# LN1 on GpSimd, paired tail rows, a spectrum by n mod 4 and loads in pieces, in a one-core H3 block

## The chip, the cores and the metric

The kernel runs on one core of one Trainium2 chip. The metric is the device time of one execution in microseconds (us); of several runs the median counts. The profile is that of one execution, and its times are counted from its first instruction.

## The reference

The kernel computes a layer of two parts for 2048 positions of width 640, in bf16: a long convolution with gating (H3), and a feed-forward part (SwiGLU).

```python
x  = A_q
q  = layernorm(x)                                  # LN1: (x - mean) / sqrt(var + 1e-5)
ks = sum(pad(k)[t:t+S] * shift_k[:, 3-t] for t in range(4))
kv = ks * v
y  = irfft(rfft(pad(kv, 2*S)) * rfft(pad(ssm_k, 2*S)))[:S] + kv * ssm_D
h  = x + q * y
z  = layernorm(h)                                  # LN2
out = h + (silu(z @ w_gate) * (z @ w_up)) @ w_down # 640 -> 1728 -> 640
```

## The kernel before, in words

**Blocks.** The 2048 positions are cut into four blocks of 512, each held as 128 partitions by 4 rows r (position 4p + r). In the program's names x, k, v and g are a block of A_q, A_k, A_v and A_ssm_k; kv is the product of the reference. The long convolution is made of spectra of single blocks: for block j the spectrum X(j) of kv and the spectrum G(j) of g are computed by matrix products with a constant WF (line L347), G is combined into windows H, and the products X(i)H(j-i) are summed into a buffer A on VectorE (`mac`, L588, L609, L612). `inverse` turns A back with a constant WI (L679 to L715 on VectorE, L727 on TensorE), multiplies by LN1's result (L741) and adds to x, which gives h. `turn_h` applies LN2 and transposes (L765, or by DMA, L758). `ffn` makes 27 products of 5 matmuls of 512 columns per block (gate and up, `whole`, L831), silu and product (L820 to L848), and the down projection (L888) with 14 pieces of 128 rows of w_down per output row; the last piece has 64 rows of data and 64 rows of zeros, in `tail` and in `wd`, which GpSimd fills (L951, L952).

**Spectra.** `transform` has two ways. `halves_of` uses that the sum over the 4 rows splits into even and odd rows: 32 matmuls of 320 columns for a spectrum, then one VectorE operation over 2560 elements. "four" uses n mod 4: 16 matmuls, then two subtractions over 1280 elements and two operations over 2560 elements. `SUM` names the spectra that go by "four": X3 and the inverses of blocks 2 and 3. Each group of matmuls ends in PSUM and is copied out by ScalarE (L339) or VectorE (L340).

**The short convolution** is done on TensorE (L567): for each row 40 matmuls with 64 contraction rows, in two halves of the partitions, against diagonal matrices `diag` made of the taps (L947). One such run of 40 is called a convolution group here, four per block.

**Layer norms.** ScalarE sums (L656) and sums of squares (L625), then `norm` makes the inverse root by nine small VectorE steps (L642 to L650, four values a partition), and `applied` scales a row on ScalarE (L667) or VectorE (L664).

**What sets the order.** The program first lists all operations with what they read and write, and then emits them in the order of a table of numbers, `ORDER`; a minus sign stands for an operation's other engine (for example ScalarE's copy on VectorE). Every engine works through its own instructions in that order, and waits where a buffer or a value isn't there. There are four PSUM buffers (`ps`), 13 large SBUF buffers (`big`), 8 of spectra (`S`) and 5 rows (`row`). Loads and DMA transposes are issued by SyncE (SP), sums by DMA (L255), some weight loads (L789) and the additions to the output (L895) by GpSimd (POOL), each queue in order.

The lines that make the two kinds of products and the tail:

```python
# L347, spectrum:      matmul(ps[:, h, 0:320], WF[:, r, c, :], src[:, r, h*320:(h+1)*320])
# L831, gate and up:   matmul(ps[:, i, :], w[:, k, off:off+128], hT[:, k, :])        # 512 columns
# L888, down:          matmul(ps[:, hf, to:to+n], tT or tail, wd[:, c, ...])         # 320 columns
```

## Time and profile before

| | before |
|---|---|
| median of 3 runs | 258.8 us (258.7 to 258.85) |
| the profiled execution's own time | 257.87 us |
| its span, first to last instruction | 256.2 us |
| TensorE (PE) busy | 247.3 us |
| VectorE (DVE) busy | 194.1 us |
| ScalarE (ACT) busy | 168.8 us |
| GpSimd (POOL) busy | 49.6 us |
| granted TensorE clock | 1.000 |

PE is the matmul side of TensorE, PEld its weight loads, which overlap with matmuls. A row of the timeline gives start, duration, engine, line, operation, output and input, how often, and in brackets the idle time before it with what ended it. The chain of waits is followed back from the last instruction; its pieces have start, duration and name. Busy times of PE count pipelined matmuls as long as they are in flight, so work is better counted by the distance of starts. "The first gate and up product" is the first L831 of block 0; it divides the program into a start, in which TensorE waits often, and the rest.

### The profile page before, as it was taken

The numbers are of one execution on the slowest core, as the hardware profiler recorded it, in microseconds if no ns is written. First come the engines' busy times: TensorE is split into PE (matmuls) and PEld (weight loads), VectorE is DVE, ScalarE is ACT, GpSimd is POOL, SyncE is SP. The second block draws the span as 40 slices with busy tenths as digits, with TensorE's granted clock in tenths as the row PEclk, the third lists the DMA queues.
The fourth block names the chain that finished last, engine by engine and source line by source line (L and its number), as shares of the span: only waits on it lengthen the run. The fifth ranks groups of instructions, "written<-read, shape, count | busy, mean of one in ns | idle before, by whom it ended". The sixth has DMA issues, their size and how long they took to land.

```text
span 256.2 us, 5180 instructions
## 1 busy us (share of the span) xinstructions
PE 247.3 (97%) x2086; PEld 149.1 (58%) x2102; DVE 194.1 (76%) x302; ACT 168.8 (66%) x289; POOL 49.6 (19%) x67
## 2 busy tenths in 40 slices
PE   6999999899999999999999999999999999999994
PEld 5676776744556477644554577544457754444672
DVE  0799999999998999998998999999989200004223
ACT  2899999895979997667579675343765344446100
POOL 6900100530300010021321610316003023000000
PEclk9999999999999999999999999999999999999999
DMA  6986998897999768699899684889915318000002
GB/s 204 397 305 142 301 144 187 254 249 179 240 269 316 171 172 153 105 208 225 220 171 175 91 199 95 144 177 252 225 32 132 75 31 102 0 0 3 0 26 77
DMA packets 51250, 41.29 MB, mean 161 GB/s; under 512 B 25429, under 2 KB 45210, under 8 KB 51226
## 3 DMA queue, kind: packets, MB, share of 16 engines
q1 hardware_dynamic: 44304, 26.53, 38.6%
q0 software_dynamic: 6912, 14.42, 30.5%
q8 instruction: 16, 0.26, 0.4%
q14 instruction: 8, 0.07, 0.1%
q10 hardware_dynamic: 10, 0.01, 0.0%
HBM read 21.94 MB, written 4.59 MB: 104 GB/s over the span
## 4 chain that ended last, share of the span: by engine, by line
PE 90%; ACT 3%; DMA 2%; DVE 2%; issue 1%; DVEq 0%; POOLq 0%
PE ps L831 45%; PE ps L888 24%; PE ps L347 10%; PE ps L727 5%; PE ps L567 4%; ACT S L339 3%; DMA row<-in_A_ssm_D_dram 2%; PE ps L426 1%; DVE tT L825 0%; DVE big L767 0%; PE ps L765 0%; DVE S L340 0%; PE ps L530 0%; DVE big L432 0%; DVE row L905 0%
## 5 line engine op out<-in xcount | busy, mean ns | idle before, releaser
L831 PE MATMUL ps<-big,big 128*128 128x512 bf16 x524 | 118.5, 379 | 0.9 <-issue 0.2
L831 PEld LDWEIGHTS <-big 128*128 128x128 bf16 x540 | 52.4, 98 | 60.4
L888 PE MATMUL ps<-wd,tT 128*128 128x320 bf16 (+2 forms) x416 | 60.2, 299 | 0.2 <-DVE tT L825 0.2
L888 PEld LDWEIGHTS <-tT 128*128 128x128 bf16 x416 | 40.6, 98 | 16.8 <-DVE tT L825 0.6
L825 DVE TENSOR_TENSOR tT<-tT,co 128x2048 bf16<-128x2048 bf16 x12 | 14.6, 1220 | 32.2 <-ACT co L820 32.1
L347 PE MATMUL ps<-big,WF 128*128 128x320 bf16 x240 | 38.3, 299 | 0.3 <-ACT co L820 0.3
L822 ACT ACTIVATE tT<-ps 128x1024 bf16<-128x1024 f32 x24 | 24.6, 1027 | 17.7 <-PE ps L831 17.6
L609 DVE TENSOR_TENSOR big<-S,S 128x2560 bf16<-128x2560 bf16 x24 | 35.0, 1483 | 1.0 <-DMA S<-big 1.0
L339 ACT ACTIVATE S<-ps 128x640 bf16<-128x640 f32 (+1 forms) x57 | 31.6, 619 | 4.1 <-PE ps L347 4.0
L820 ACT CAST co<-ps 128x1024 bf16<-128x1024 f32 x24 | 24.2, 1013 | 13.7 <-PE ps L831 12.8
L347 PEld LDWEIGHTS <-WF 128*128 128x128 bf16 x240 | 22.9, 97 | 11.3 <-issue 1.6
L255 POOL DMA_DIRECT2D S<-big x9 | 10.9, 1208 | 82.7 <-DVE sm L644 28.3
L625 ACT ACTIVATE row<-big 128x640 bf16<-128x640 bf16 x32 | 23.4, 734 | 2.8 <-DMA big<-row 2.7
L612 DVE TENSOR_TENSOR S<-S,big 128x2560 bf16<-128x2560 bf16 x16 | 23.7, 1486 | 0.2
L667 ACT ACTIVATE row<-big,sm 128x640 bf16<-128x640 bf16 x22 | 19.5, 918 | 3.1 <-DVE sm L650 3.1
L895 POOL DMA_DIRECT2D out_dram<-row x12 | 12.8, 1356 | 15.8 <-ACT row L894 15.8
L741 DVE SCALAR_TENSOR_TENSOR row<-row,ps 128x640 bf16<-128x640 bf16 x16 | 12.9, 818 | 2.9 <-PE ps L727 2.3
L894 ACT CAST row<-ps 128x640 bf16<-128x640 f32 x12 | 8.0, 692 | 10.8 <-PE ps L888 9.0
L255 POOL DMA_DIRECT2D S<-S x5 | 6.6, 1328 | 41.5 <-ACT S L339 33.2
L567 PEld LDWEIGHTS <-T 64*128 64x128 bf16 x640 | 11.3, 110 | 3.5 <-issue 3.0
L567 PE MATMUL ps<-diag,T 64*128 64x64 bf16 x640 | 12.6, 194 | 0.0
L588 DVE TENSOR_TENSOR big<-S,S 128x2560 bf16<-128x2560 bf16 (+1 forms) x10 | 12.2, 1218 | 0.0
(87 smaller groups left out, 247.2 us busy)
## 6 DMA issues: line engine op xcount, KB each, us to landing
S<-big POOLq DMA_DIRECT2D x9, 640.0 KB, 6.6
big<-in_B_w_up_dram SPq DMA_DIRECT2D x10, 320.0 KB, 5.0
big<-in_B_w_gate_dram SPq DMA_DIRECT2D x10, 320.0 KB, 5.3
S<-S POOLq DMA_DIRECT2D x5, 640.0 KB, 9.1
big<-in_A_ssm_k_dram SPq DMA_DIRECT2D x4, 640.0 KB, 9.3
big<-in_A_q_dram SPq DMA_DIRECT2D x4, 640.0 KB, 6.7
big<-in_A_v_dram SPq DMA_DIRECT2D x4, 640.0 KB, 8.6
wd<-in_B_w_down_dram SPq DMA_DIRECT2D x1, 2080.0 KB, 15.2
```

Of the source, the lines that this page charges most:

```text
L255: nc.gpsimd.dma_start(out=to(), in_=what(), accum_op=ALU.add, max_dma_last_dim=2 * D * 2)
L339: plan.add("act", 700 if n else 430, lambda: nc.scalar.activation(dst(), src(), ACT.Copy, scale=by), [ps], [part], (), ("dve", 820 if n el ...
L347: nc.tensor.matmul(ap(ps)[:, h, 0:NH], ap(WF)[:, r, c, :], ap(src)[:, r, h * NH:(h + 1) * NH], start=(first and i == 0), stop=(last and i ...
L567: nc.tensor.matmul(out()[:, b, c, :], k, ap(diag)[at, c, t, :], start=(t == 0), stop=(t == 3))
L609: dve(1490, lambda b=b, xs=xs, hs=hs: nc.vector.tensor_mul(flat2(b), X.part(xs), H.part(hs)), [X.at(xs), H.at(hs)], [b], [A.b])
L612: f(A.part(dst), A.part(dst), flat2(b))
L625: act(825, lambda r=r, junk=junk: nc.scalar.activation(ap(junk), ap(x)[:, r, :], ACT.Square, scale=D ** -0.5, accum_out=sm(s, 1)[:, r:r + ...
L667: nc.scalar.activation(ap(row), ap(x)[:, r, :], ACT.Identity, bias=sm(s, 5)[:, r:r + 1], scale=sm(s, 4)[:, r:r + 1])
L820: act(1010, lambda ps=ps: nc.scalar.copy(ap(co)[:, at:at + 2, :], ap(ps)), src, [(co, gi % 2)])
L822: act(1010, lambda ps=ps: nc.scalar.activation(ap(tT)[:, c:c + 2, :], ap(ps), ACT.Silu), src, [done(range(c, c + 2), ROWS)])
L831: nc.tensor.matmul(ap(ps)[:, i, :], ap(w)[:, k, off:off + P], ap(hT)[:, k, :], start=(k == 0), stop=(k == KT - 1))
L888: nc.tensor.matmul(ap(ps)[:, hf, to:to + n], t, ap(wd)[:, c, col + (hf - hs[0]) * NH:col + (hf - hs[0]) * NH + n], start=(c == order[0]), ...
```

## The change

- LN1 of blocks 1 to 3 goes by `apart`, five GpSimd operations, one of them a power with exponent -0.5 from a new constant `root`, in place of nine VectorE steps. Block 0's LN1 and every LN2 stay.
- The down projection has 13 whole pieces. The 64 rows of the last piece are loaded twice into `wd`, to partitions 0 to 63 and 64 to 127; `tail` is half as long, with the second half of the positions in the upper partitions, and four matmuls with 64 contraction rows serve two output rows (`halves`, L900 of the new program). Odd blocks go through the pieces backwards. The fills with zeros go.
- The spectrum of block 2's kv goes by "four".
- A_k and A_v of block 0 are loaded in two parts, A_ssm_k of block 0 in parts of two and three column groups, and WF in two.
- The last output row is still cut into 384 and 256 columns, now with the 256 last.
- `ORDER` is a new table. In it block 0's keys come before its filter, 16 of the 20 operations that make `diag` go from GpSimd to VectorE, and the convolution groups of block 2 stand among block 0's gate and up products; before, they stood ahead of the first of them.

```diff
-SUM = {'X3': 'four', 'i2': 'four', 'i3': 'four', 'G3': 'four'}
+SUM = {'X3': 'four', 'i2': 'four', 'i3': 'four', 'G3': 'four', 'X2': 'four'}
-LASTCUT = 2
+LASTCUT = 384
+GPIECES = ((0, 2), (2, KT))
 ORDER = [
-    21, 0, 20, 2, 1, 14, 4, 5, 6, 7, 19, 3, 47, 45, 51, 46, 48, 49, 53, 17, -51, 8, 27, 52, 29, 28, -31, 25, 201, 23, -27,
+    0, 4, 15, 16, 1, 2, 5, 6, 9, 3, 7, 24, 28, 12, 17, 32, 22, -14, 29, 30, -34, 31, 23, 14, 26, 54, 11, -28, 34, 19, 57,
...
+    root = fixed([P, R], FP32, "root")
-    tail = fixed([P, BLK], BF16, "tail")
+    tail = fixed([P, BLK // 2], BF16, "tail")
...
-    def load_t(src, j):
+    def load_t(src, j, n=1):
         b = new("ld")
-        load(MB, 5120, lambda: nc.sync.dma_start(out=rd(b), in_=block(src, j)), [b])
+        for lo in range(0, R, R // n):
+            load(MB // n, 5120 // n, lambda lo=lo: nc.sync.dma_start(out=rd(b)[:, lo:lo + R // n, :], in_=block(src, j)[:, lo:lo + R // n, :]),
+                 [(b, frozenset(range(lo, lo + R // n)))])
         return b
...
+    def apart(s):
+        v = nc.gpsimd
+        def go():
+            v.tensor_mul(sm(s, 6), sm(s, 2), sm(s, 2))
+            v.tensor_sub(sm(s, 3), sm(s, 1), sm(s, 6))
+            v.tensor_scalar(sm(s, 3), sm(s, 3), EPS, None, op0=ALU.add)
+            v.tensor_tensor(sm(s, 4), sm(s, 3), ap(root), op=ALU.pow)
+            v.tensor_mul(sm(s, 5), sm(s, 2), sm(s, 4))
+        plan.add("pool", 5500, go, [root], [s])
...
-        norm(s)
+        if plan.block:
+            apart(s)
+        else:
+            norm(s)
         return s
...
-            act(600, lambda ps=ps: nc.scalar.activation(ap(tail)[0:64, :], ap(ps)[0:64, 0, :], ACT.Silu), [(ps, 0)], [done_tail(ROWS)], [tT])
-            act(590, lambda ps=ps: nc.scalar.copy(ap(co)[0:64, 1, :], ap(ps)[64:P, 0, :]), [(ps, 0)], [(co, 1)])
-            dve(420, lambda: nc.vector.tensor_mul(ap(tail)[0:64, :], ap(tail)[0:64, :], ap(co)[0:64, 1, :]), [(co, 1)], [done_tail(ROWS)], [tT])
+            for i in range(2):
+                at, cols = slice(i * H2, (i + 1) * H2), slice(i * half_of, (i + 1) * half_of)
+                act(395, lambda ps=ps, at=at, cols=cols: nc.scalar.activation(ap(tail)[at, :], ap(ps)[0:H2, 0, cols], ACT.Silu), [(ps, 0)], [(tail, i)], [tT])
+                act(390, lambda ps=ps, at=at, cols=cols: nc.scalar.copy(ap(co)[at, 1, 0:half_of], ap(ps)[H2:P, 0, cols]), [(ps, 0)], [(co, 1 + i)])
+            dve(290, lambda: nc.vector.tensor_mul(ap(tail), ap(tail), ap(co)[:, 1, 0:half_of]), [(co, 1), (co, 2)], [tail], [tT])
...
+        order = list(range(NC_FULL))[::1 if j % 2 == 0 else -1]
+        for pair in ((ROWS[0], ROWS[2]), (ROWS[1], ROWS[3])):
...
+            def both(rows=rows):
+                i = ROWS.index(rows[0][0])
+                for k in range(2):
+                    for b, (r, ps, cuts, last) in enumerate(rows):
+                        ps, hf, n, col = cuts[k]
+                        at = slice(b * H2, (b + 1) * H2)
+                        nc.tensor.matmul(ap(ps)[:, hf, 0:n], ap(tail)[at, i * P:(i + 1) * P], ap(wd)[at, NC_FULL, col:col + n],
+                                         start=j % 2 == 1, stop=j % 2 == 0, skip_group_check=True)
...
-    plan.add("pool", 600, lambda: nc.gpsimd.memset(ap(tail)[64:P, :], 0.0), [ident], [(tail, "zero")])
-    plan.add("pool", 600, lambda: nc.gpsimd.memset(ap(wd)[64:P, NC_FULL, :], 0.0), [ident], [(wd, "zero")])
```

The first place is TensorE at the end of block 0's down projection (`tT_85` holds 13 pieces of the product of silu and up, `tail` the last; `ps_93` to `ps_96` are the four PSUM buffers). Before:

```order
L888 MATMUL ps_96<-wd,tT_85 128x320
L888 LDWEIGHTS tail
L888 MATMUL ps_96<-wd,tail 128x320
L888 LDWEIGHTS tail
L888 MATMUL ps_96<-wd,tail 128x320
L888 LDWEIGHTS tT_85
L888 MATMUL ps_95<-wd,tT_85 128x320
```

And in the changed program:

```order
L915 MATMUL ps_94<-wd,tT_85 128x320
L900 LDWEIGHTS tail
L900 MATMUL ps_95<-wd,tail 128x320
L900 LDWEIGHTS tail
L900 MATMUL ps_93<-wd,tail 128x320
L900 LDWEIGHTS tail
L900 MATMUL ps_95<-wd,tail 128x320
L900 LDWEIGHTS tail
L900 MATMUL ps_93<-wd,tail 128x320
L915 LDWEIGHTS tT_85
```

Two tail matmuls for one output row become four, with 64 contraction rows each, for two output rows; there are 8 such groups in the program.

The second place is ScalarE in the start, in the changed program: `S_65` takes block 0's X, `S_64` block 0's G, `big_72` is the transposed filter of block 1. Before, the 16 copies into `S_64` were all made, by both engines, ahead of the first into `S_65`.

```order
L344 ACTIVATE S_65<-ps_96 128x320
L344 ACTIVATE S_65<-ps_95 128x320
L344 ACTIVATE S_64<-ps_93 128x320
L344 ACTIVATE S_64<-ps_94 128x320
L344 ACTIVATE S_64<-ps_96 128x320
L435 COPY big_72<-ps_95 128x640
L344 ACTIVATE S_64<-ps_96 128x320
```

G's second half of the columns is now copied behind X's first half.

The third place is GpSimd's queue at LN1 of block 2 (`sm_102`), in the changed program; before, the queue had none of the five L660 to L664.

```order
L925 DMA out_dram<-row_88 128x640
L660 TENSOR_TENSOR sm_102<-sm_102 128x4
L661 TENSOR_TENSOR sm_102<-sm_102 128x4
L662 TENSOR_SCALAR sm_102<-sm_102 128x4
L663 TENSOR_TENSOR sm_102<-sm_102,root 128x4
L664 TENSOR_TENSOR sm_102<-sm_102 128x4
L925 DMA out_dram<-row_90 128x640
L925 DMA out_dram<-row_89 128x640
L256 DMA big_73<-row_90 128x640
```

They stand between the additions of block 0's output rows; behind them come two more of these additions and the sums by DMA into h of block 2.

145 lines of the change are left out of this document (75 added, 70 removed), and 78 rows, old and new, of the table ORDER.

## The prediction

> **What bounds the kernel now.** I read the page's shares and its slices first, then busy times by stage, then the chain of waits, and at last the timeline where TensorE waits.
>
> ```profile
> PE 247.3 (97%) x2086; PEld 149.1 (58%) x2102; DVE 194.1 (76%) x302; ACT 168.8 (66%) x289; POOL 49.6 (19%) x67
> DVE  0799999999998999998998999999989200004223
> ACT  2899999895979997667579675343765344446100
> ```
>
> ```profile
> core 0: us, PE busy (x) PEld busy (x) DVE busy (x) ACT busy (x) POOL busy (x), PEclk, DMA share, GB/s
> 6.00:18.00 12.00, 11.48 (x252) 8.98 (x252) 9.91 (x23) 10.55 (x28) 6.68 (x16) 1.00 1.01 384
> 18.00:34.00 16.00, 15.48 (x264) 11.34 (x256) 15.96 (x30) 15.83 (x35) 1.28 (x1) 1.00 0.82 205
> 34.00:51.00 17.00, 16.35 (x271) 12.28 (x267) 16.28 (x39) 15.75 (x30) 3.36 (x4) 1.00 0.93 193
> 51.00:89.00 38.00, 37.79 (x198) 19.63 (x201) 36.83 (x48) 33.86 (x62) 4.82 (x5) 1.00 0.98 240
> 150.00:208.00 58.00, 57.84 (x347) 33.94 (x348) 48.30 (x73) 29.74 (x42) 10.79 (x11) 1.00 0.66 139
> ```
>
> TensorE is the bound of the whole, but not of every stage. From 18 to 51 us ScalarE is busy 31.58 of 33 us and VectorE 32.24. The reader is to see that this start isn't set by matmuls alone. From 51 us on TensorE hardly stops. So I split the time at the first gate and up product. The chain of waits gives that point and the prices of the work behind it:
>
> ```profile
> 50.83 0.32 PE ps L831
> ...
> 123.43 0.79 PE ps L567 x40
> 124.23 0.32 PE ps L831
> 124.55 0.05 issue
> 124.60 2.97 PE ps L831 x13
> 127.57 0.80 PE ps L567 x40
> ...
> 161.97 10.74 PE ps L831 x49
> 172.71 0.05 issue
> 172.76 10.74 PE ps L831 x49
> ...
> 193.02 15.26 PE ps L888 x112
> ...
> 252.67 0.56 DVE row L905
> ```
>
> A 512-column matmul costs (172.76 - 161.97)/50 = 0.2158 us (the "issue" stands for a matmul without a record), one of 320 columns 15.26/112 = 0.1363. From one convolution group to the next 4.14 us pass, with 15 gate and up matmuls between by the program (14 recorded, one under "issue"), 3.24 us; so a group of 40 among such matmuls costs 0.90. Its weight loads are spaced closer:
>
> ```profile
> 123.36 0.75 PEld L567 LDWEIGHTS <-T 64*128 64x128 bf16 x40 [0.42 <-issue]
> ```
>
> With 0.11 us for the last, (0.75 - 0.11)/39 is 0.0164 a matmul, 0.65 for 40. The other 0.25 is what going to 64 contraction rows and back costs; the 0.42 idle shows that the loads can't run ahead there.
>
> Count of the work behind 50.83, with the numbers of matmuls from the program: 540 gate and up 116.5, 448 down 61.0, 80 spectrum and 64 inverse 19.6, 4 convolution groups 3.6; together 200.7. To 252.67 are 201.8 us. So 1.1 us idle is all that can be won there without taking work away. Half of it stands in one place:
>
> ```profile
> 144.78 1.04 PE L347 MATMUL ps<-big,WF 128*128 128x320 bf16 x6 [0.29 <-ACT co L820]
> 146.05 2.89 PE L888 MATMUL ps<-wd,tT 128*128 128x320 bf16 x20 [0.23 <-DVE tT L825]
> ```
>
> **The change part by part.**
>
> **Block 2's spectrum:** 16 matmuls fewer, 16 x 0.1363 = 2.18 us of TensorE. Behind the split, though, the new order has 16 matmuls of other spectra that stood ahead of it before: 80 spectrum matmuls before and after. So the saving is taken in the start, where other engines set the end. VectorE gets two subtractions more, off TensorE's path.
>
> **Paired tails:** 32 tail matmuls, 32 x 0.1363 = 4.36 us, become 8 groups. In a group two pairs run side by side, 2 x 0.1363 = 0.27, if halves overlap as in the convolution, where 64 columns pass every 0.0164 us and one half alone needs a fifth of a 320-column matmul, 0.027. The way into 64 rows and back adds 0.25. I take 0.52 a group, 4.2 in all: a saving of 0.2. Bounds: without the way in and out 2.2 saved; with no overlap, 4 x 0.1363 + 0.25 = 0.80 a group, 2.0 lost. The Trainium skill, page "TensorEngine Tiling (Array Packing)", promises up to 2x for at most 64 contraction rows in "Theoretical Speedup"; by that alone the sum would be 2.0 better. The same page says in "Key Properties" that a change of the tiling mode drains the engine, which speaks against so short groups; the 0.25 of this trace agrees with the drain.
>
> **Moved convolution:** 8 groups instead of 4 stand behind the split, two of them directly behind another in each half of the count. 8 x 0.65 + 6 x 0.25 = 6.7 against 3.6: 3.1 more there. I take it in full; at worst each pays its own way in and out, 0.5 more.
>
> **The start:** what sets the split is ScalarE, which copies nearly all of the spectra out of PSUM. Its steps, from start to start:
>
> ```profile
> 6.71 1.88 ACT L430 COPY big<-ps 128x640 bf16<-128x640 bf16 x3 [3.82 <-PE ps L426]
> 16.55 0.72 ACT L625 ACTIVATE row<-big 128x640 bf16<-128x640 bf16 x1
> 17.27 0.72 ACT L625 ACTIVATE row<-big 128x640 bf16<-128x640 bf16 x1
> 17.98 2.74 ACT L339 ACTIVATE S<-ps 128x320 bf16<-128x320 f32 x7
> ```
>
> ```profile
> 43.49 2.46 ACT L339 ACTIVATE S<-ps 128x640 bf16<-128x640 f32 x4
> 45.32 1.15 DVE L664 TENSOR_SCALAR row<-big,sm 128x640 bf16<-128x640 bf16 x3
> 45.83 1.30 ACT L576 CAST big<-ps 128x640 bf16<-128x640 f32 x2
> 46.99 1.12 POOL L952 MEMSET wd<- 64x640 bf16 x1
> 47.07 1.54 DVE L664 TENSOR_SCALAR row<-big,sm 128x640 bf16<-128x640 bf16 x1
> 49.53 0.69 ACT L767 COPY big<-ps 128x640 bf16<-128x640 bf16 x1 [1.11 <-PE ps L765]
> ```
>
> A copy of 320 columns takes 0.39, of 640 columns 0.60, a convolution's copy 0.64. Up to the last copy of block 0's transposed h, ScalarE gets 6 copies of 320 more (+2.3), 5 of 640 fewer (-3.0), 3 convolution copies fewer (-1.9), and two copies of transposes more (+1.2): -1.4. The fourth L664 took 1.54 us where the others took 0.4, while GpSimd filled `wd`; the fill goes, and with it the 1.11 that ScalarE waits before the last copy. Its sums for LN1 of block 0 move into the time in which it waits for the filter. The first bytes come in smaller pieces:
>
> ```profile
> 5.92 1.15 PEld L426 LDWEIGHTS <-big 128*128 128x128 bf16 x20 [1.39 <-DMA big<-in_A_ssm_k_dram]
> 7.67 0.70 PEld L530 LDWEIGHTS <-big 128*128 128x128 bf16 x11 [0.60 <-DMA big<-in_A_k_dram]
> ```
>
> The first 640 KB were there at 5.9, the next at 7.7. Half of the keys may be there a us earlier, but the sums need x, which is second and comes at 7.7; by then ScalarE has done 1.4 us of copies, as much as before by 8.1. I take no gain from the pieces. The split moves by -1.4 - 1.1 = -2.5, to 48.3. Bounds: 1.4 us earlier still, if the early copies count in full (46.9); 50.5, if the eight G copies behind X's first half (8 x 0.39 = 3.1 before X is whole) find no work of TensorE ready, and 2.2 of the 2.5 are lost.
>
> **LN1 on GpSimd:** 27 VectorE steps go, 0.2 each as these two stand apart, 5.4 us of an engine that TensorE rarely waits for. Fifteen GpSimd operations come:
>
> ```profile
> 44.26 0.16 DVE L645 TENSOR_TENSOR sm<-sm 128x4 f32<-128x4 f32 x1
> 44.45 0.16 DVE L646 SCALAR_TENSOR_TENSOR sm<-sm 128x4 f32<-128x4 f32 x1
> ```
>
> ```profile
> L942 POOL TENSOR_TENSOR row<-ident 128x64 bf16<-128x64 bf16 x1 | 0.3, 307 | 0.1
> ```
>
> A power isn't in the trace. Five at 0.31 are 1.5; the fill's 1.12 each would be 5.6. The nearer row is the tensor operation of 64 columns. In the new order some ten ScalarE instructions of 0.6 to 1.0 us stand between the last sum and the first use of block 2's, so 5.6 is hidden, and I cost it at nothing; without that cover it is 1.5 for each of three blocks. Queued behind it are two additions to the output and the sums into h, which ScalarE's row buffers wait for.
>
> **Idle and end:** the VectorE chain to the last inverse gets shorter, so I take 0.6 instead of 1.1 idle behind the split (-0.5), with 0 and 3 as bounds. The last addition has 256 instead of 384 columns: from the 0.56 above to about two thirds of it, -0.1 to -0.2; its output DMA is shorter too. I take -0.2.
>
> **Sum:** split -2.5, convolution +3.1, tails -0.2, idle -0.5, end -0.2: -0.3 us. The profiled execution, 257.87 (span 256.2), would take 257.6; it ran 0.9 under the median of 258.8. On the median that is 258.5. A measurement of this kernel can tell about 0.2%, 0.5 us, from no change.
>
> **The rivals.** First, a faster tail and start: the 64-row groups pay no way in and out between 320-column matmuls (-2.0 more), or the early keys count in full (-1.4 more). For it: the start's DMA is what the first copies wait for, 3.82 us. Against it: 0.25 at each group in the trace. With either alone 257.1 or 256.5, with both 255.1. (The first half of this is what the 2x of the Trainium skill's page "TensorEngine Tiling (Array Packing)", section "Theoretical Speedup", would give.)
>
> Second, slower: ScalarE's queue in the start. G's second half is copied behind X's first, so X is whole only when 24 copies of 320 are through instead of 16, and VectorE's products and the inverse wait for it. If the split comes later than 48.6, the moved convolution, which is then paid behind it, is more than what was gained. At 50.5 the sum is +1.9: 260.7. For it: VectorE is full there too; against it: ScalarE has less to do in all.
>
> Third, slower: a sum by DMA or the GpSimd norms hold up VectorE's products of block 1, and TensorE waits for the inverse; 1 to 2 us, 259.5 to 260.5. For it: the DMA share is 0.98 from 51 to 89 us; against it: VectorE has fewer steps.
>
> Fourth, the moved convolution does what such a move would be for: it fills waits of TensorE behind the split. Against it: there are only 1.1 us of them.
>
> **How the numbers follow.** The forecast, an even trade, 0.42, with its own range 257.6 to 259.4; the first rival with the fourth 0.36; the second 0.14, the third 0.08. The forecast's 0.42 falls to faster 0.13, same 0.20 and slower 0.09; the first gives faster 0.34 and same 0.02; the last two slower 0.22. That makes faster 0.47, same 0.22, slower 0.31. The range reaches to both rivals: low end 255.6, high end 260.6.
>
> **What would show it.** Right: a first gate and up product near 48.3; 6.7 us of convolution behind it; about 0.5 us between the down matmuls around a tail group, with idle weight loads before it. Wrong: a split before 47 or after 49.5; tail groups under 0.35; TensorE waiting for VectorE between 70 and 150 us; a ScalarE LN1 use that waits for GpSimd.

## The result, and the profile after

The changed kernel is slower: 261.57 us in the median of 5 runs (260.38 to 264.44), against 258.7 for the kernel before on the same chip; the ratio is 1.0104 [1.0082, 1.0126]. On another chip it came out at 260.48, ratio 1.008 [1.0048, 1.0112]. The forecast was 258.5 with a range up to 260.6. The profiled execution of the changed kernel took 260.66 us (span 258.9), that of the kernel before 257.87 (256.2), so 2.7 us of span are to be explained. All ratios below compare with the kernel before on the same chip and leave disturbed runs out, so that they can differ from a quotient of medians.

The page of the changed kernel, busy times and two rows of its 40 slices:

```profile
PE 248.0 (96%) x2086; PEld 146.3 (57%) x2086; DVE 192.9 (74%) x285; ACT 172.2 (67%) x303; POOL 65.2 (25%) x67
DVE  2699999969799999996999999999977300012313
PEclk9799999999999999999999999999999999999999
```

Two things are new. VectorE, which stood at 8 or 9 tenths up to three quarters of the span, now has slices at 6 and 7, and GpSimd is busy 15.6 us longer with as many instructions (67). And the clock row has a 7 in its second slice. The same by stages (core, stretch, length, then each engine's busy time, granted clock, DMA share and GB/s):

```profile
6.00:18.00 12.00, 9.52 (x211) 7.22 (x209) 9.34 (x32) 9.79 (x27) 0.00 (x0) 0.86 1.02 341
...
47.80:89.00 41.20, 39.26 (x350) 20.83 (x348) 37.36 (x38) 33.70 (x53) 12.50 (x13) 1.00 0.94 210
150.00:208.00 58.00, 57.01 (x342) 32.82 (x340) 50.00 (x68) 34.49 (x57) 24.73 (x17) 1.00 0.71 136
```

From 6 to 18 us the granted clock is 0.86, where it was 1.00. From 150 to 208 GpSimd is busy 24.73 us instead of 10.79. Behind the split TensorE now stands still 1.94 us up to 89 us, where it stood 0.21 before, and VectorE stands still with it: 3.84 us, where it was 1.17. The waits of TensorE, largest first (what it waited for, us in total, times, longest):

```profile
PE ps L431 <- DMA big<-in_A_ssm_k_dram: 2.2, 1, 2.2
PE ps L745 <- DVE big L697: 1.9, 1, 1.9
PE ps L745 <- ACT co L835: 1.0, 1, 1.0
PE ps L570 <- ACT big L579: 0.8, 1, 0.8
```

The first is in the start. The other three lie behind the split, at 72.9, 191.5 and 122.9 us: in the inverse of block 1, in the inverse of block 3, and in a convolution group that waits for ScalarE. The chain of waits says what stands behind them (start, length, what):

```profile
46.11 9.20 DMA S<-S
55.44 1.50 DVE big L612
...
60.16 10.12 DMA S<-big
70.37 2.91 DVE S L615 x2
...
113.75 9.18 DMA S<-big
...
176.90 7.19 POOL sm L660
...
255.94 0.43 DVE row L935
```

Before, 90% of this chain was TensorE. Now three sums by DMA of 9 to 10 us each are links of it, and 7 us of one GpSimd operation on four values a partition. (A sum by DMA is a transfer, issued by GpSimd, that adds what it brings to what stands at its target.)

**Where the 2.7 us are.** The first gate and up product stands at 47.79 instead of 50.83:

```profile
47.79 1.24 PE L846 MATMUL ps<-big,big 128*128 128x512 bf16 x5
```

That is -3.0. From there to the last addition are 208.15 us (255.94 - 47.79) instead of 201.8: +6.3. The end behind it is 2.96 instead of 3.53: -0.6. Of the +6.3, 3.2 are the convolution (8 groups, 6.76 by the distance of starts, instead of 3.6 for 4) and -0.6 the tails (8 groups of 0.46 to 0.49, 3.7 to 3.9, instead of 4.36). The three waits cost 2.09, 1.01 and 1.15 us by the starts of the matmuls around them, in order of time, 4.25 in all against 1.1 idle before: +3.1. The sum is 5.7; the remaining 0.6 is spread over many matmuls and not assigned.

### The profile page after: what moved, and what is told of

It is laid out like the page before. It is cut to its first block, busy times and chain, and to the rows that moved or that the text cites. A ratio compares the mean times of both kernels' runs of the same rounds, so it can differ in the third digit from the quotient of the medians.

```text
span 258.9 us, 5184 instructions
## 1 busy us (share of the span) xinstructions
PE 248.0 (96%) x2086; PEld 146.3 (57%) x2086; DVE 192.9 (74%) x285; ACT 172.2 (67%) x303; POOL 65.2 (25%) x67
## 4 chain that ended last, share of the span: by engine, by line
PE 38%; issue 20%; DMA 13%; DVE 10%; ACT 10%; POOL 7%; SPq 0%; POOLq 0%; DVEq 0%; ACTq 0%
PE ps L846 16%; PE ps L915 11%; DMA S<-big 7%; ACT S L344 6%; DMA S<-S 4%; PE ps L570 3%; PE ps L745 3%; POOL sm L660 3%; DMA big<-in_A_ssm_k_dram 2%; PE ps L352 2%; DVE S L591 2%; POOL S L256 2%; DVE tT L840 1%; PE ps L431 1%; DVE S L615 1%
## 5 line engine op out<-in xcount | busy, mean ns | idle before, releaser
L846 PE MATMUL ps<-big,big 128*128 128x512 bf16 x540 | 121.0, 379 | 0.0
L915 PE MATMUL ps<-wd,tT 128*128 128x320 bf16 (+2 forms) x416 | 59.2, 299 | 0.0
L352 PE MATMUL ps<-big,WF 128*128 128x320 bf16 x224 | 37.4, 299 | 1.0 <-ACT S L344 0.5
L344 ACT ACTIVATE S<-ps 128x640 bf16<-128x640 f32 (+1 forms) x62 | 32.6, 609 | 7.1 <-PE ps L352 7.0
L352 PEld LDWEIGHTS <-WF 128*128 128x128 bf16 x224 | 21.2, 97 | 13.2 <-issue 2.6
L615 DVE TENSOR_TENSOR S<-S,big 128x2560 bf16<-128x2560 bf16 x17 | 25.2, 1490 | 4.1 <-DMA S<-big 4.1
L685 ACT ACTIVATE row<-big,sm 128x640 bf16<-128x640 bf16 x20 | 17.6, 921 | 6.2 <-DVE sm L653 4.0
L925 POOL DMA_DIRECT2D out_dram<-row x12 | 12.2, 1177 | 16.4 <-ACT row L924 16.4
L570 PEld LDWEIGHTS <-T 64*128 64x128 bf16 x640 | 12.1, 113 | 4.4 <-issue 4.3
L745 PEld LDWEIGHTS <-WI 128*128 128x128 bf16 x96 | 9.1, 98 | 8.5 <-DVE big L697 2.4
L256 POOL DMA_DIRECT2D S<-S x3 | 3.9, 1296 | 38.3 <-ACT S L344 38.3
```

The lines of the kernel that those rows point to most:

```text
L256: nc.gpsimd.dma_start(out=to(), in_=what(), accum_op=ALU.add, max_dma_last_dim=2 * D * 2)
L344: plan.add("act", 700 if n else 430, lambda: nc.scalar.activation(dst(), src(), ACT.Copy, scale=by), [ps], [part], (), ("dve", 820 if n el ...
L352: nc.tensor.matmul(ap(ps)[:, h, 0:NH], ap(WF)[:, c, r, :], ap(src)[:, r, h * NH:(h + 1) * NH], start=(first and i == 0), stop=(last and i ...
L570: nc.tensor.matmul(out()[:, b, c, :], k, ap(diag)[at, c, t, :], start=(t == 0), stop=(t == 3))
L615: f(A.part(dst), A.part(dst), flat2(b))
L685: nc.scalar.activation(ap(row), ap(x)[:, r, :], ACT.Identity, bias=sm(s, 5)[:, r:r + 1], scale=sm(s, 4)[:, r:r + 1])
```

## The experiments

The theory behind the result: the parts priced from TensorE's rows are right, and the loss is three waits behind the split, two of them at a sum by DMA that lands late, one at GpSimd's norm of block 3. Rivals: GpSimd's norms hold the whole queue, the sums behind them included; the load of the down weights (2.08 MB, issued at 52.70, before at 68.37) takes the DMA engines from the sums; the granted clock, 0.991 in this execution, makes the difference by itself. A last question was whether the tail groups pay what was priced.

### Is it GpSimd's norms?

`norm_vector` puts the three LN1 norms back on VectorE, as nine steps each.

```diff
-        if plan.block:
+        if plan.block in ():
             apart(s)
```

> The changed kernel with one thing undone: the LN1 norms of blocks 1 to 3 are again the nine VectorE steps each, put between VectorE's big operations where these stood idle or short of the first use; GpSimd computes nothing after the start. Theory A (GpSimd's small operations are held up by VectorE's two-input products; that made 13.8 us out of the last norm and the 0.99 us wait of TensorE at 191.6): this wait is gone, and the time falls by 0.8 to 1.2 us against the changed kernel, to 260.4 to 260.8. If GpSimd's norms also held up the sums by DMA, the first wait (1.92 at 72.9) and the second (0.84 at 122.9) shrink too, and it falls by 2 to 3. Rival (the norm is off the path, the sums by DMA set all three waits): within 0.4 us of the changed kernel, and the wait near 191 stays, now for VectorE, which has 27 steps more, some 4 us in all.

Measured: 260.0 us, ratio 1.0057 [1.0033, 1.008]. Waits of TensorE behind the split, the longer ones (one of 0.5 us for a load of w_up is left):

```profile
PE ps L745 <- DVE big L697: 1.6, 1, 1.6
PE ps L570 <- ACT big L579: 1.0, 1, 1.0
```

The wait in block 3 is gone. Against the changed kernel's two ratios, 1.0104 and 1.008, that is 0.5 or 0.2%, and the interval of the second, taken on another chip, overlaps with this one: the trace shows the wait's 1 us, while the times hardly do. The two others stay, and the three sums by DMA take 9.0, 10.05 and 9.32 us as before. So the norms cause the third wait and do not hold the sums.

`pool_writes` asks how GpSimd loses its time there: five fills in place of the five operations, which read nothing; LN1's mean and scale of blocks 1 to 3 are left out.

```diff
-            v.tensor_mul(sm(s, 6), sm(s, 2), sm(s, 2))
-            v.tensor_sub(sm(s, 3), sm(s, 1), sm(s, 6))
...
+            v.memset(sm(s, 1), 1.0)
+            v.memset(sm(s, 2), 0.0)
...
```

> The changed kernel with the five GpSimd operations of each LN1 norm of blocks 1 to 3 replaced by five fills of the same 128x4 tiles, which only write: LN1's mean and scale of these blocks are left out. If GpSimd is held off while VectorE reads two inputs, because both read through one interface: fills take 0.1 to 0.3 us each even while VectorE multiplies without a break, the first one of block 3 too (7.97 us for a multiplication there), and ScalarE's wait for the norm near 188 goes. If GpSimd is held off by the descriptors of the three DMAs that it issued just before: the first fill of block 3 still takes several us. If VectorE shuts GpSimd out for writes too: fills of about 1.5 us, as the reading operations.

GpSimd's timeline in the changed kernel, the first operation of block 1's norm, two of block 2's, then block 3's norm (start, duration, engine, line, operation, tiles, how often):

```profile
63.74 0.38 POOL L660 TENSOR_TENSOR sm<-sm 128x4 f32<-128x4 f32 x1 [2.38 <-ACT row L671]
...
117.42 3.23 POOL L660 TENSOR_TENSOR sm<-sm 128x4 f32<-128x4 f32 x1
120.73 0.19 POOL L661 TENSOR_TENSOR sm<-sm 128x4 f32<-128x4 f32 x1
...
176.10 7.97 POOL L660 TENSOR_TENSOR sm<-sm 128x4 f32<-128x4 f32 x1
184.16 1.50 POOL L661 TENSOR_TENSOR sm<-sm 128x4 f32<-128x4 f32 x1
...
188.97 0.94 POOL L664 TENSOR_TENSOR sm<-sm 128x4 f32<-128x4 f32 x1
```

ScalarE's first use of it there:

```profile
189.95 1.73 ACT L685 ACTIVATE row<-big,sm 128x640 bf16<-128x640 bf16 x2 [2.28 <-POOL sm L664]
```

And VectorE in the same stretch:

```profile
174.38 4.29 DVE L612 TENSOR_TENSOR big<-S,S 128x2560 bf16<-128x2560 bf16 x3
178.59 1.49 DVE L615 TENSOR_TENSOR S<-S,big 128x2560 bf16<-128x2560 bf16 x1
...
184.11 1.49 DVE L697 TENSOR_TENSOR big<-S 128x2560 bf16<-128x2560 bf16 x1
```

GpSimd with fills in their place:

```profile
183.68 0.10 POOL L660 MEMSET sm<- 128x4 f32 x1 [3.08 <-ACT row L628]
```

L661, an operation on four values a partition, takes 0.19 us where VectorE has nothing to do (at 121) and 1.5 us, the length of one of VectorE's products, where it works without a gap. The fills take 0.10 beside such products, and the wait of TensorE there is gone. So these operations wait for SBUF reads while VectorE reads two operands. The Trainium skill, page "SBUF — State Buffer", section "Who interferes with whom", says so: a VectorE instruction with two SBUF inputs contends with a GpSimd instruction that reads SBUF, not with one that only writes. The trace agrees for the 1.5 us ones.

The first one of block 3, 7.97 us, is longer than that. It ends at 184.07, at the first pause that VectorE makes since it began (184.01 to 184.11). Block 2's, 3.23 us, ends with VectorE's pause at 120.59, and in `sums_vector` (below), where that pause comes at 121.29, it takes 6.05 us. So its length follows VectorE's unbroken row. But the row alone doesn't make it long: block 1's took 0.38 us inside such a row. Block 1's had stood 2.38 us behind GpSimd's last DMA issue, while two DMA issues stand right ahead of the 3.23 and three right ahead of the 7.97. The long ones are thus seen only right behind DMA issues and beside an unbroken row; why it takes both stays open. The fills don't test it, since they stood 3.08 us behind an issue.

The kernel itself took 262.59 in its two runs, 1.0148 [1.0119, 1.0176], slower than the changed kernel: in the profiled execution the first sum by DMA took 12.43 us, TensorE waited 4.66 for block 1's inverse, and behind this wait the granted clock stood at a half from 77.3 to 80.7 us. That is no answer on the norms, but a first sign that the length of these sums sets the time.

### Is it the load of the down weights?

`wd_later` moves this load and its two tail pieces behind block 3's filter load.

```diff
 ORDER = [
-    ..., -285, 346, 358, 359, 285, 466, 211, 462, 469, ... 342, 384, 209, 210, 297, ... 385, 648, 307, ...
+    ..., -285, 346, 358, 359, 285, 466, 462, 469, ... 342, 384, 297, ... 385, 648, 211, 209, 210, 307, ...
```

> The changed kernel, but the load of the down weights (2.1 MB) is issued behind the load of block 3's filter, at about 72 us instead of 52.7. Theory B (two sums by DMA, 9.2 and 10.1 us long, came late because they shared the DMA engines with this load, and TensorE's 1.92 us wait at 72.9 is VectorE's wait for them): the sum issued at 60.2 takes 6 to 7.5 us instead of 10.1, the wait falls under 0.8, and the time by 1.0 to 1.5 us. Rival (the sum is held up by GpSimd, which computes the norm of block 1 from 63.7 to 68.7): it still takes 9 to 10 us, the wait stays, no gain. Against both: the load now lands near 88; if it lands after 91.4, TensorE waits for it before the first down product and the gain is lost.

Measured: 260.99 us, ratio 1.0074 [1.0044, 1.0104]. The sum issued at 60.85 took 5.62 us instead of 10.1, and the wait in block 1's inverse is gone: the load was what this sum shared the DMA engines with. But in this execution, 262.79 us and the third longest of twelve, other transfers came late: the next sum took 11.1, and TensorE waits for transposes by DMA and for the load itself instead:

```profile
PE ps L352 <- DMA big<-big: 1.9, 2, 1.2
...
PE ps L915 <- DMA wd<-in_B_w_down_dram: 0.2, 1, 0.2
```

Behind these waits the clock fell to a half a second time (94.8 to 98.2 us). The runs differ much: the five with a mean clock of 0.999 or 1.000 took 258.3 to 259.3 us, the others, at 0.987 to 0.993, 260.5 or more. The ratio can't be told apart from the changed kernel's, so this place for the load gains nothing that the median shows. The DMA engines are nearly full from 47.8 to 89 in the changed kernel (share 0.94 above, before 0.98); in `wd_later` their share falls to 0.4 and 0.2 from 58.7 to 71.8 us and is full behind that. Whether the load fits into this gap without harm wasn't tried.

### Is it the sums by DMA?

`sums_vector` makes two sums on VectorE: block 1's X sum (in the changed kernel by DMA at 46.11) and block 2's accumulator sum (at 113.75). `sum_x1` and `sum_acc2` do one of them each.

```diff
-    369, 353, 362, 368, 363, 276, 471, -275, 283, ...
+    369, 353, 362, 368, 363, 276, 471, 274, 283, ...
...
-    ..., 425, 519, 520, 583, -510, 682, ...
+    ..., 425, 519, 520, 583, 509, 682, ...
```

> The changed kernel with two sums taken from GpSimd's DMA queue and done by VectorE: that of block 1's X at 46.1 us (9.2 us until it landed, VectorE idle 2.07 for it) and that of block 2's accumulator at 113.8 (9.2 us, VectorE idle 2.36). Theory B (VectorE waits for late sums, and TensorE for VectorE): VectorE spends 1.49 us on each instead of its waits, the sum at 60.2 lands in 6 to 9 us as it has less beside it, TensorE's waits at 72.9 (1.92) and 122.9 (0.84) shrink to under 1.0 and to 0, time 1.0 to 2.0 us under the changed kernel. Rival (VectorE is as full as TensorE there, so that 3 us more of work come out at its inverse): the waits stay and the time changes by under 0.4.

> The changed kernel with only the sum of block 1's X (46.1 us) on VectorE. If it is the one that set the loss (VectorE's products of block 1 wait for it, and in other executions it took 7.4 to 12.4 us): TensorE's wait at 72.9 goes, the time falls by 1.5 to 2.5 us and the spread of the runs shrinks to under 2 us; TensorE's 0.84 us wait at 122.9 stays. If the sum is late by nothing of weight: within 0.5 us of the changed kernel.

> The changed kernel with only the sum into block 2's accumulator (113.8 us) on VectorE. If each sum costs what TensorE waits for it: 0.8 us under the changed kernel, and the wide spread stays, as the sum at 46.1 still goes by DMA. If this is the one that set the loss: 1.5 us or more, with a small spread.

| | median us (lowest to highest) | ratio |
|---|---|---|
| changed kernel, two chips | 261.57 (260.38 to 264.44), 260.48 | 1.0104 [1.0082, 1.0126], 1.008 [1.0048, 1.0112] |
| X sum on VectorE | 258.66 (257.8 to 260.2) | 1.0025 [1.0003, 1.0047] |
| accumulator sum on VectorE | 259.02 (257.7 to 261.8) | 1.0026 [1.0004, 1.0049] |
| both | 257.65 (257.31 to 257.97) | 0.9955 [0.9942, 0.9968] |

With both, two of TensorE's four waits above are left:

```profile
PE ps L431 <- DMA big<-in_A_ssm_k_dram: 2.6, 1, 2.6
PE ps L745 <- ACT co L835: 1.0, 1, 1.0
```

With the X sum alone the first wait is gone and the second (0.9) stays; with the accumulator sum alone the first stays (1.7, its sums took 9.19 and 9.88) and the second is gone. Both are worth 1.25 to 1.5%, 3.2 to 3.9 us: somewhat more than the two waits take in the profiled execution of the changed kernel, 2.8 us by the list and 3.1 by the starts. Each alone gives 0.55 to 0.8%, and its interval ends about where the changed kernel's on the other chip begins. What goes too is the spread of the times, 4 us for the changed kernel and 0.7 without the two sums; block 1's X sum was seen to take 7.4, 9.2 and 12.4 us in executions of `fill_same`, the changed kernel and `pool_writes`. This settles that the sums by DMA are the main loss, and gives a kernel faster than both.

What makes these sums long is only in part shown. The trace records every packet of a queue: the X sum, issued at 46.11, moves its first packet at about 50.7 and lands at 55.3; the ones issued at 60.16 and 113.75 move their first packets at about 64.8 and 118.7. So about half of the time passes ahead of the first packet. For the second this is when the packets of the down weights' load end, and in `wd_later`, without that load, 1.7 us pass instead of 4.6. For the first it is open, since the engines were nearly idle from 49.5 to 50.5.

### Is it the clock?

The second slice at 7 tenths lies at 8.8 to 12.2 us. TensorE's timeline there, changed kernel:

```profile
4.96 1.47 PE L533 MATMUL ps<-ident,big 128*128 128x128 bf16 x20
8.58 0.51 PE L431 MATMUL ps<-ident,big 128*128 128x128 bf16 x4 [2.15 <-DMA big<-in_A_ssm_k_dram]
9.03 1.25 PE L570 MATMUL ps<-diag,T 64*128 64x64 bf16 x40
```

A convolution group takes 1.25 us there instead of some 0.8. `filler` puts 36 matmuls without use ahead of it, so that TensorE doesn't stand still; `fill_same` gets the same cover from as many instructions as before, by wider matmuls.

```diff
+    spin(36)
     first("k0")
```

> The changed kernel with 36 matmuls on constants more (2.0 us), on TensorE between the transposes of the keys and those of the filter, where it waited 2.15 us for the filter; the granted clock stood at 0.5 from 8.8 to 12.2 us behind this wait. Theory C (the wait makes the clock fall, and with it the convolution and the transposes take some 1.4 us longer): granted clock 1.000, the same work from 8.6 on is done 1.2 to 1.5 us earlier, and if the start hangs on it the first gate and up product moves from 47.8 to 46.4 to 47.0. Rival (ScalarE is busy with its sums until 12.2 anyway): it moves by 0.4 at most. In either case, if the first wait at 72.9 is set by the sums by DMA and VectorE, what is won before it is waited there again, and the time changes by under 0.4 us; else it falls by 1 us.

```diff
-    spun = spin(WARMUP[1])
+    spun = spin(WARMUP[1] // 2, 2 * P)
...
-    first("k0")
+    spin(WARMUP[1] // 2, 4 * P); first("k0")
```

> The changed kernel with TensorE kept busy in the wait for the filter, but with as many instructions as before: of the 16 warming matmuls of 128 columns, 8 of 256 stay where they are and 8 of 512 (1.7 us) stand between the transposes of the keys and of the filter. Theory C: granted clock 1.000, the convolution from 9 us on at full speed, first gate and up product 0.5 to 1.4 us earlier, time 1 to 2 us under the changed kernel (259.5 to 260.5) and closer together. Rival (the clock costs nothing, since ScalarE or VectorE's sums by DMA set what follows): within 0.5 us of it. The filler of 36 more matmuls lost 1.29 us at 12.1 and 2.80 us at 41.4 in TensorE waits without a releaser, each beside a 16 KB transfer of instructions: if that came from the moved place of its instructions, these waits are gone here; if from the filling itself, they are here again.

`filler` kept the clock at 1.000 and cost time all the same: 263.29, ratio 1.0203 [1.0181, 1.0226], split at 51.33. TensorE in its timeline:

```profile
10.88 1.26 PE L570 MATMUL ps<-diag,T 64*128 64x64 bf16 x74 [0.20 <-DVE big L435]
13.43 0.27 PE L570 MATMUL ps<-diag,T 64*128 64x64 bf16 x6 [1.29 <-issue]
...
40.71 0.72 PE L352 MATMUL ps<-big,WF 128*128 128x320 bf16 x4
44.23 0.99 PE L352 MATMUL ps<-big,WF 128*128 128x320 bf16 x6 [2.80 <-issue]
```

Two new waits, 1.29 and 2.80 us, have no releaser. Ahead of each ends a transfer of 16 KB on the queue that the profile calls instruction. With as many instructions as before they are gone (`fill_same`):

```profile
6.72 1.91 PE L959 MATMUL ps<-const-bfloat16-1.0 128*128 128x512 bf16 x7
...
8.79 0.76 PE L570 MATMUL ps<-diag,T 64*128 64x64 bf16 x40
```

Clock 0.999, the group at 0.76, split at 46.80 instead of 47.80: 259.86 us, ratio 1.0052 [1.0022, 1.0083]. So the clock's dip costs about 1 us of the start, by one execution of each; the ratio overlaps with the changed kernel's 1.008. The runs of `sums_norm3` (below) fit it: 255.5 to 256.0 us at a mean clock of 1.000, 256.6 to 257.5 at 0.991 to 0.993, as one such dip gives, and 258.0 and 258.4 at 0.987, as two give. In the changed kernel's profiled execution the dip is no part of the 6.3 behind the split, since the clock is 1.00 there.

`all_three` joined `norm_vector`, `wd_later` and `filler`, and had `filler`'s two waits (0.82 and 2.23) and a split at 52.14: 264.78, ratio 1.0259 [1.0231, 1.0288]. It says nothing on how the parts add up.

> The three edits together: norms on VectorE, the down weights later, 36 filling matmuls. If the three act apart from each other (A, B and C), the gains add up: 3 to 4 us under the changed kernel, about 257.7 to 258.6, level with the kernel before. If one wait stands behind the other and takes up what is won, it is 1 to 2 us under the changed kernel only.

`after_again` is the changed kernel once more, to have it beside the next ones: 260.48, and TensorE's waits again 2.0, 1.0 and 0.7, split 47.80. Its runs don't show that the clock alone sets their length: the two longest (262.42 and 263.89) had 0.986, but one with 1.000 took 260.48 and the shortest (258.96) had 0.992. Where a dip comes behind the split, in the traces of `pool_writes` and `wd_later`, it follows a wait for a late transfer, so that such a transfer can cost clock as well.

> The changed kernel itself once more, as the base for the other three on one chip. Its runs so far had a granted clock of 0.986 to 0.993 and went from 260.4 to 264.4 us. If the half clock near 9 us is what makes them differ (theory C), runs with a higher mean clock are the shorter ones; if it is something else, clock and time have nothing to do with each other.

`g_first` takes the other way to that wait: x is loaded behind the filter's pieces, by one entry of the table moved; `g_first_norm` adds `norm_vector`.

```diff
-    0, 4, 15, 16, 1, 2, 5, 6, 9, 3, 7, 24, 28, 12, 17, 32, 22, -14, 29, 30, -34, 31, 23, 14, 26, ...
+    0, 4, 15, 16, 1, 2, 5, 6, 9, 3, 7, 24, 28, 12, 32, 22, -14, 29, 30, -34, 31, 23, 17, 14, 26, ...
```

> The changed kernel with one transfer moved: x is loaded behind the two pieces of block 0's filter instead of ahead of them. The filter, 8.5 us in the changed kernel, should be there at 6.8 to 7.4 us and x at 8.5 instead of 7.8. Theory C: TensorE waits under 1 us, the clock stays at 1.000, the first gate and up product moves 0.5 to 1.4 us forward, time 1 to 2 us under the changed kernel. Rival: ScalarE's sums of x begin 0.7 us later and push its copies of the spectra, so the start is no shorter: within 0.5 us, or 0.5 slower.

> The filter ahead of x and the LN1 norms on VectorE together. If both act and apart from each other: 2 to 3 us under the changed kernel, 258.5 to 259.5, near the kernel before. If the sums by DMA hold what the start gains, only what the norms gave (1.2 us).

TensorE begins on the filter at 6.83 us instead of 8.58 and the clock is 1.000, but then it waits 0.83 us for `diag` and 1.3 for a copy (1.1 and 1.7 in `g_first_norm`); split 48.01 and 48.66, times 260.35 (1.0097 [1.0063, 1.013]) and 261.48 (1.0101 [1.0064, 1.0139]). No gain: in the start the next engine is late at once.

### The parts together

`three_again` has all norms on VectorE, the filling and both sums; `sums_norm3` both sums and block 3's norm alone; `sums_norm3_fill` the filling with it.

```diff
-        if plan.block:
+        if plan.block in (1, 2):
             apart(s)
```

> Norms on VectorE, the filling with as many instructions as before, and the two sums on VectorE, together. If the three waits stand apart: 1.2 + 0.7 + 1.0 to 2.0 us under the changed kernel, 256.8 to 258, that is under the kernel before. If VectorE is now the bound of the blocks (4.3 us of norm steps and 3 us of sums more): no better than the norms alone, 259 to 260.

> Both sums on VectorE, and of the LN1 norms only block 3's, where VectorE's products leave GpSimd no pause. Theory A: TensorE's 0.98 us wait at 188.5 goes, and the time falls by 0.7 to 1.0 us against the kernel with both sums moved (257.65), to 256.7 to 257.0. Rival (nine steps more delay VectorE's own chain to the last inverse as much): no gain.

> The same, and TensorE kept busy ahead of the filter with as many instructions as before. If the start hangs on the clock: the first gate and up product at 46.8 instead of 48.1 and another 0.7 to 1.2 us, 255.7 to 256.3. If block 1's products on VectorE set what follows: the 1.2 us are waited at the first inverse behind it, and it is equal to the one without.

| | median us | ratio |
|---|---|---|
| three_again | 258.07 | 0.9984 [0.9967, 1.0001] |
| sums_norm3 | 256.87 | 0.995 [0.993, 0.9971] |
| sums_norm3_fill | 255.86 | 0.9911 [0.989, 0.9932] |

With all three norms on VectorE as well as the two sums, TensorE waits 0.99 for block 1's inverse again: there VectorE itself is the last, and 18 small steps of blocks 1 and 2 are better off on GpSimd. With block 3's alone, its wait goes, but against `sums_vector` (0.9955) the gain isn't resolved. With the filling the split is at 46.78 instead of 48.40 in the profiled runs, and TensorE has no wait behind the split that its list shows (all of these, the longest, are in the start):

```profile
PE ps L959 <- PEq L1089: 0.8, 1, 0.8
PE ps L352 <- ACT S L344: 0.5, 1, 0.5
PE ps L352 <- DVE big L578: 0.3, 1, 0.3
...
```

Its stage behind the split, to hold against the changed kernel's 39.26 of 41.20 and 37.36:

```profile
46.80:89.00 42.20, 42.20 (x368) 22.84 (x366) 42.02 (x42) 36.87 (x62) 13.37 (x13) 1.00 0.92 197
```

TensorE 42.20 of 42.20 us and VectorE 42.02. This kernel is 2.3 us faster than the one before on the same chip (258.32).

### The tails and the fill

`tail_in_turn` is `sums_norm3_fill` with the two matmuls of one half of a tail group before those of the other, to see whether the order decides if the halves overlap.

```diff
-                for k in range(2):
-                    for b, (r, ps, cuts, last) in enumerate(rows):
+                for b, (r, ps, cuts, last) in enumerate(rows):
+                    for k in range(2):
```

> The version with both sums, block 3's norm on VectorE and the filling, with one order changed: in each of the 8 tail groups the two 64-row matmuls of one row pair stand before the two of the other, instead of in turns, so that only the second and third can run side by side. If the halves run side by side when they alternate (four matmuls in 0.37 us, two times 0.136 and the switch): the group takes 0.14 us longer, 8 x 0.14 = 1.1 us, 257.0 instead of 255.9. If they run one behind the other either way: 0.37 us as before, and no change.

A group in the changed kernel, with its weight loads behind it, and then in this one:

```profile
106.04 0.45 PE L900 MATMUL ps<-wd,tail 64*128 64x320 bf16 x4
106.42 1.53 PE L915 MATMUL ps<-wd,tT 128*128 128x320 bf16 x10
```

```profile
106.04 0.11 PEld L900 LDWEIGHTS <-tail 64*128 64x128 bf16 x4 [0.26 <-issue]
106.41 0.66 PEld L915 LDWEIGHTS <-tT 128*128 128x128 bf16 x6 [0.27 <-issue]
```

```profile
102.95 0.45 PE L900 MATMUL ps<-wd,tail 64*128 64x320 bf16 x4
103.33 1.53 PE L915 MATMUL ps<-wd,tT 128*128 128x320 bf16 x10
```

0.38 us from start to start in both, 255.65 us, ratio 0.9899 [0.9873, 0.9924], not to be told from 0.9911. Four such matmuls one behind another would be 4 x 0.1363 = 0.55, so the halves overlap, and in either order. The starts of single matmuls tell more, and are alike in all eight groups of both kernels: two start within 7 ns, the other two 0.14 to 0.15 us behind them, and the next matmul of full height 0.23 behind these, where 0.136 is usual. The first pair, too, comes 0.09 to 0.10 later than a matmul of the usual kind would. So 0.38 is 0.15 for the first pair and 0.23 for the second with the way out, and the way in and out costs 0.19 together. By the semaphore updates the one that starts third in `tail_in_turn` is the first half's second matmul: the other half's first has started ahead of it, out of the program's order.

`before_fill` goes the other way: the kernel before, with GpSimd's fill of the zero rows of `wd` moved from 47.0 to about 12.7 us. It tests the -1.1 that the forecast gave to this fill.

```diff
-    ... 349, 350, 16, 269, 468, ...
+    66, -44, 63, 15, 16, 67, 44, ... 349, 350, 269, 468, ...
```

> The kernel before with one order changed: GpSimd fills the zero rows of the down weights at 12.7 us, right behind the zero rows of the tail, instead of at 47.0. My prediction's price of 1.11 us for this fill (VectorE's fourth scaling of block 0's rows took 1.54 instead of 0.4 us while it ran, and TensorE and ScalarE waited 1.1 for it): the first gate and up product moves from 50.8 to 49.7, and the end by 0.8 to 1.1, 257.2 to 257.6. Rival (the scaling was slow for another reason, or the sums by DMA behind it take up what is won): within 0.3 us of the kernel before.

Measured: 257.82 us, ratio 0.9962 [0.9948, 0.9977], that is 1.0 us (0.6 to 1.3), as much as expected. But the trace, of the longest of its five runs, shows the price in another place only in part: TensorE's wait of 0.62 is gone and 0.57 us are won there, half of the 1.11 that were booked, and the fourth scaling still takes 0.97 us without the fill beside it (1.54 before). The split is at 50.95 and not earlier than 50.77, because the first spectrum matmul comes at 10.00 instead of 9.26. Where the rest of the 1.0 us comes from isn't shown.

## Why the prediction was wrong

- **The start: -2.5 forecast, -3.0 measured.** Split 47.79, inside its bounds (46.9 to 50.5). The second rival (ScalarE's queue, split at 50.5) did not come. The parts are less sure than the sum: the fill was worth 1.0 us in the times of `before_fill` but 0.57 in its trace, and a clock dip that wasn't thought of took about 1 us (`fill_same`). With the dip's 1.0 added and the fill's 0.6 or 1.0 taken off, some 3.0 to 3.4 us (an estimate) were won in ScalarE's queue or by the early keys, where 1.4 was booked; how the two share it was not tried. That the sum came out near is in part luck.
- **The moved convolution: +3.1 forecast, +3.2 measured.** Right. The fourth rival, that it fills waits, was wrong in the way foreseen.
- **The tails: 0.52 a group forecast, 0.46 to 0.49 measured** (0.38 from start to start, and 0.08 to 0.11 that the matmul ahead of it takes longer). Saving 0.5 to 0.7 us instead of 0.2. The idle weight loads, 0.26 and 0.27, are the way in and out that was looked for; by the starts it costs 0.19 instead of the 0.25 that was taken.
- **The end: -0.2 forecast, -0.6 measured.** The last addition takes 0.43 us instead of 0.56 as forecast; the rest behind it is shorter by more than assumed.
- **Idle behind the split: the step that failed.** "The VectorE chain to the last inverse gets shorter, so I take 0.6 instead of 1.1 idle behind the split (-0.5), with 0 and 3 as bounds." Measured are the three waits, 4.25 us, +3.1 where -0.5 was booked, and over the upper bound. The chain that was counted on did not get shorter where it mattered: fewer VectorE steps do not help where VectorE itself waits for a transfer (two of the waits), and the last inverse waited for GpSimd's norm (the third). Before, block 1's X sum was under way nearly as long as after (issued 46.26, 9.6 us; after 46.11, 9.2), but VectorE's first product that needs it came late, since norm, kv and block 0's products stood ahead of it. The product, and a later addition of another sum that waited for nothing:

```profile
61.94 4.29 DVE L609 TENSOR_TENSOR big<-S,S 128x2560 bf16<-128x2560 bf16 x3
...
72.40 1.49 DVE L612 TENSOR_TENSOR S<-S,big 128x2560 bf16<-128x2560 bf16 x1
```

  The X sum had landed at 55.9: 6 us of slack. In the new order of the changed kernel VectorE comes to the product before the sum lands and waits, and so it does at two later additions of sums by DMA:

```profile
55.44 1.50 DVE L612 TENSOR_TENSOR big<-S,S 128x2560 bf16<-128x2560 bf16 x1 [2.07 <-DMA S<-S]
...
70.37 2.89 DVE L615 TENSOR_TENSOR S<-S,big 128x2560 bf16<-128x2560 bf16 x2 [1.70 <-DMA S<-big]
...
122.95 1.49 DVE L615 TENSOR_TENSOR S<-S,big 128x2560 bf16<-128x2560 bf16 x1 [2.36 <-DMA S<-big]
```

  At the X sum the new order spent the slack. The two later sums had landed only 0.1 us ahead of their use before as well (72.3 for 72.40, 124.2 for 124.29), but VectorE was at work until then; now it has nothing left to do and waits 1.70 and 2.36 us. The forecast counted steps and neither slack nor what VectorE would do meanwhile.
- **LN1 on GpSimd: "I cost it at nothing", wrong for block 3.** The prices taken, 1.5 or 5.6 us for the five, came from operations that met no VectorE product; block 3's took 13.8 us (176.10 to 189.91), and the cover of ten ScalarE instructions, argued from block 2, doesn't hold there. It cost the third wait, 1.15 us by the starts; in the times of the runs this isn't resolved. In blocks 1 and 2 it cost TensorE nothing that the waits show, as forecast.
- **The rivals.** The third one was the case: a sum by DMA and the GpSimd norms hold up VectorE's products and the inverse, "1 to 2 us, 259.5 to 260.5". Its mechanism and its place (between 70 and 150 us) were right; with 0.08 its chance was too small, and its price too low by half, since it had one wait and there were three. The argument against it, that VectorE has fewer steps, was the same one that failed above.

## What to carry to other kernels

When a new order moves a consumer forward, look up when its input lands and not only how much the engine has to do: the slack of every transfer between issue and first use is part of the price. Where DMA engines are full over a stretch, a long sum by DMA on the path comes late and also makes the time uncertain, and two 1.5 us instructions on an engine with some room can be cheaper. Small operations moved to GpSimd were cheap here where VectorE left gaps, and dear beside its unbroken products, so decide block by block.

## What the runs showed of the hardware that was not expected

- GpSimd operations on 128x4 values took 0.19 to 0.23 us with VectorE idle, 1.3 to 1.5 beside VectorE products without a gap, and 3.23, 6.05 and 7.97 for three that stood right behind DMA issues and beside a whole row of these; fills took 0.10. The contention that the page of the Trainium skill named above states is borne out; the waits over several products are more than it speaks of, and as block 1's 0.38 us shows they don't come with every such row.
- A sum by DMA of 640 KB took 5.6 us with little beside it (in `wd_later`) and 7.4 to 12.4 us elsewhere, from execution to execution. With two of them on VectorE the spread of the times fell from 4 us to 0.7.
- A matmul on one half of the rows started ahead of one that stood before it in the program and used the other half (`tail_in_turn`, inferred from the semaphore updates).
- One wait of 2.15 us behind 1.5 us of transposes took the granted clock to a half for 3.4 us, and this cost about 1 us of the start. The Trainium skill, page "TensorE: Matmul & The Clock Gate", section "What's actually happening", gives a window of 3413 ns, free-running, and at least one such window without work as the condition. The length of the dip agrees. The wait alone is shorter than the window, and by the section "Part 4: PE-mode transpose" transposes don't count as busy in the same way. But other dips here had no transposes ahead of them: in `wd_later` one followed 3.41 us with 1.91 us idle and real matmuls in the rest, in `all_three` one with 2.18 idle. In the other direction `filler`'s wait of 2.80 us, of which at most 1.54 lay in one such stretch, when these are counted from the trace's first clock step, left the clock at 1.000. So here about half a window of idle was enough, and the measurement decides; where exactly the limit lies isn't shown.
- 36 matmuls more in the start, 72 instructions with their weight loads, made TensorE wait 1.29 and 2.80 us with no releaser, each behind a 16 KB instruction transfer. That it is the fetch of instructions is inferred; that it comes with their number is shown by the filling with the same count.
